# Linear attention block and gated MLP on one core: statistics, loads and issue orders rearranged at the start, in the middle and at the end

## The chip, the cores and the metric

The kernel runs on one core of a Trainium2 chip. A core has TensorE (PE in the profile; PEld are its weight loads), VectorE (DVE), ScalarE (ACT), GpSimd (POOL) and SyncE (SP), each with its own instruction stream; they meet at semaphores. SP and ACT issue the DMAs here. The metric is device time in microseconds, lower is better.

## The reference

The sequence has 2048 tokens of width 512. Two residual blocks follow one another:

```
h   = x + A(layernorm(x))           # layernorm without weights, eps 1e-5
A:    q, k, v = split(xn @ wqkv)    # 32 heads of width 16
      phi(t) = where(t > 0, t + 1, exp(t)) + 1e-6
      o = (phi(q) @ (phi(k)^T v)) / (phi(q) . sum_s phi(k) + 1e-6)
      A = o @ wo
out = h + B(layernorm(h))
B:    z = gelu(hn @ w_in)           # 512 -> 1792, tanh form
      z1 = z[:, :896];  z2 = layernorm(z[:, 896:])
      g = w_sp @ z2 + b_sp          # w_sp is 2048 x 2048 over tokens
      B = (z1 * g) @ w_out          # 896 -> 512
```

## The kernel before, in words

Tokens lie in 16 tiles of 128; four tiles make a group (tg). Everything stays in SBUF. The program first records every operation with its engine, reads and writes (class `_Prog`), and then issues them on each engine in an order that is written out by hand: `ORDER` is a packed list of all operation numbers. So the order of the calls in the code says what depends on what, and the list says when each engine does it. An engine takes its operations strictly in that order, and one that waits holds up all behind it. The matmuls, activations and DMAs go through helpers, so many different operations carry the line of one helper (L402 matmuls, L421 activations, L432 loads, L435 DMA transposes, L533 norms); tiles tell them apart.

**Head.** Pool sets constants, among them `warm`, which the warm-up matmuls read. x is loaded in pieces (x0 is tile 0, x4-5 two tiles), wk is the K third of wqkv in two halves, wq the Q third. `k_unit` handles two tiles: mean and variance of each (`stats`, two DVE operations), `rstd` on Pool (add eps, power -0.5, and for tiles from 6 on the negated mean), the norm, and a transpose to xnT: tiles 0 to 5 by PE (`tr`) and an ACT copy (`cp`), the others by a DMA transpose on SP (`xt`). Then the K product (k0, k1, ...), `phi` to pk (exp on ACT, min and a scalar_tensor_tensor, "stt", on DVE), and the accumulation C += xn^T pk in four PSUM banks (C0, C1, ..., one for each tile). This gives the context matrix with v folded in later: ct is the copy of C, kv multiplies it with wv and masks heads, m multiplies that with wo. `q_unit` makes phi(q) of two of four channel blocks of a group, transposed (pqT). `z_unit` sums pk over tokens (zsum, zsel, zc).

**h stage.** For each group, `den` is the denominator; ACT takes its reciprocal as exp(-ln), SP spreads it over partitions in four DMAs (`spread`), and DVE multiplies pqT by it (`pqmul`). For each tile, h = x + pqT^T m: PE product (h0, h1, ...) in one of three banks, DVE add with the row sum (L726), ACT square with its sum (hSq), Pool `moments` (three operations of 128x1) and power, DVE norm (hn), and a DMA transpose to hnT (ht).

**z stage.** z2 products (z2 0 to 15, one for a tile; gelu on ACT, layernorm) and z1 products (transposed, 7 for a group). w_sp is transposed by DMA in row blocks of 128, whole or as two halves of 1024 columns.

**Gating.** One Strassen step over pairs of token groups (`cell`): DVE combines blocks of w_sp into t and of z2 into s, PE multiplies, DVE gates with z1. `mo` is the output product of a tile, a DVE add of h (L797) and the store.

Of the kernel before, what the change touches and what calls it, by code (L numbers as in the profile page):

```python
# [7 lines left out]
BF16 = mybir.dt.bfloat16  # L8
# [5 lines left out]
EARLY = 2  # L14
SEM_NS = 45.0
ORDER = "c-jTQ1war05Cgz%k0L5!pjZfsf`}+8SQvny7zikW0d{wHcXxMpcXxMpcX#)lGhC1k8ITc~;D*e|f;P$yccg?PlEVQhU;qdq6>`7>X^<A_;fk#AL{8*_7jmO0d=Q9Y2tsj`Ks_X(K1!l4N}~!YAsh0*8+nlrzQ_+h1fw8Ip$y8xAC(b>02DwWG(bZ%Mk7>3G(r%H7*t0`v_~g&Kw-op4n@!mVQ7K~R6`BKBLPn6j4tSk?r4st=z;PmhlQwsa16&tj6hA)!YI^6YIH+S^g>HSq6I3V4ieD{^RWPn&>DNN7j3W)`!O10Fb>Hu7K^b2%div&a1e(u5#!MteXtUJ(GUHx9EULogE0g{F$|M10V}WyZP5->Fd4Hk3&$`OM=%EiFc8P_7)S945Ag);)Ikr>TGKEcb1@HVuo`Qz37atkGqDcqu?1VP4Lh(MCvgHhu?xF#3LCHyr*Q@sa2{uI1?O-PS8)lKaSbo<40rGxH*pKsaRX2B7ccP-js#QiHeTT^UgHZs<1U=|4sY-k_i!H{@g8aU13%$FBPo8sC!}L~{(>`8GZj-Z6EiR)U74KUkc{7vi!SuyZ=~TL1hO>!n1w;i&8#fSJoKgy^U|03S%%Rp&zh`2e->kLmS9O1U^bRz3^Q{hBN@Vi3}7e=(T%~Z$S{^;Ef!`2He@*SaT8mz6=T_n+3C(4^k6A=W=?vtH;1qfhcbdiSeu(!jg8oaTiBY7S)G+wnN8S~b=Zt?Y{Nt*u?7$EFo&@(hjRqSavYCvJmWc^fttnz3{n+#Wm|S*J9cLjCvYLRvM!Hu5f}3qSFj$Nb2?YDsEVrx`>{PcuqWFpfmPXp^;t|Mw1oXRfCD**BUw_VR9eBB!I_-MrQF5c3{e@aVp)ai6i+iu;VP#Hl~<%HsG=&ViYlwBq7<#c?8sgm#nBwYNu12p+{QCJ%RSu7Wt_rUoXzdr!8KgVIh@ONT+een&yL!_d0ft^j8UwrDNfZDuNtbU1l3k8C8~~+bcvT)Uv*Vaw|IrO`G}ACghkXt?bTJ?)k~e#MV-`51Jp<T)l+@dPrcPpuh>Yhd52edjZgWE*Lj!sc!T%(fH(PuZ@G{A`J4y%f}i-AU)VrR^^2z8OeF^;Q)>O;JO1TAKIB2Z<X2wcH@@cwCf9N9q@z;kJDv1{7wN1tN~sfc(Me`dGr20GGRaMul|>NMSlN_aUTUJ;`bl?vWDa@AQ)!h>Ih99}xBQe}{_;^?`Ko{lD!sBQpK>Wcg;ZFhHC!##TqCqli!@$KH9@VkOp~-i1GQaaG)Ut#SW~r1Q#4USv_m^JS-Uh=(=<v$wOAuHT`e?Qd$n9MG)F5nOmj6;v$R@kv|IDERvR^6OSDeEwLp7xK>M^_TeL}=wLu4UNQZSqTeVGRwO>bdO2>3sXLL@NbXn(hMaOkPS9M)CbW^u<LML@ccXdzq^-z!WSWom!&-Fqt^;&QARv+|HpOoJI=$~L2jF!>d%q*Gx&{zG`Fa6aw$-XPOxmpTKZBFK3j^=D>EVE^?l$OeJn~P<&Y?jtOE1hMs?3TlFS|0N;cYCK?=4Bq{Y5C00LaeBTS~2rAZ_97~me&ecuobaV7GdSBpaoixmA2wm!NRPJ1z4n&vl3Rw3R|2-TMdi17>l(^R@tgpHH)$Yd#a1Nrm_}p4^+}B+AF=+7ge|0s%kZ@mesa8mS{=#AF{cVy#"
# [236 lines left out]
def bass_sequential_preLN__linear_attn_block__mixer_gmlp__prompt_kernel(  # L253
# [93 lines left out]
    rc = [g.sbuf(f"rc{b}", o_r + GW * 4 + b * GW * 2, [GW], BF16) for b in range(2)]  # L347
    r16 = [g.sbuf(f"r16{b}", o_xn + b * KD * GW * 2, [KD, GW], BF16) for b in range(NG)]
# [79 lines left out]
    def pool(fn, reads, writes, ns, **k):  # L428
        return g.add("POOL", fn, reads, writes, cost=ns, lat=60, **k)
# [13 lines left out]
    pool(lambda p: p.memset(epst[:, 0:1], EPS_DEN), [], [epst], 80, bias=1e6)  # L443
# [17 lines left out]

    wq = A_wqkv.rearrange("(c p) f -> p c f", p=P)
# [91 lines left out]
    def phi(dst, b, w=2):  # L554

        e, t = e_t[ecnt[0] % NE][:, 0:w, :], psum[:, b:b + w, :]
        ecnt[0] += 1
        act_exp(e, t, ACT.Exp, w * GW)
        dve(lambda v: v.tensor_scalar(e, e, 1.0, EPS_PHI, op0=ALU.min, op1=ALU.add), [e], [e], w * GW, acc=4)  # L559
        dve(lambda v: v.scalar_tensor_tensor(dst, t, 1.0 + EPS_PHI, e, op0=ALU.add, op1=ALU.max),  # L560
            [t, e], [dst], w * GW, ps=True)

    def warmup(n):
# [328 lines left out]
```

## Time and profile before

| what | value |
|---|---|
| median of 5 runs | 236.63 us (236.34 to 237.02) |
| profiled execution, its own time | 237.08 us |
| its span, first to last instruction | 235.2 us |
| PE / DVE / ACT / POOL busy | 227.6 / 150.7 / 92.3 / 54.0 us |
| HBM read / written | 7.47 / 2.10 MB |

A line of the timeline or of the groups gives start, duration in us, engine, line of the kernel, operation, output <- inputs, shape and count; in brackets stands the idle time of the engine before it and what ended it. The chain of waits follows the work that ended last back to the start. The profiled execution is one, the median is of others.

### The profile page before, as it was taken

To read this page: it belongs to the slowest core of one execution; us is meant where nothing else is said; L and a number is where in the kernel's file an instruction comes from. 1 tells how busy PE (TensorE), PEld (TensorE's weight loads), DVE (VectorE), ACT (ScalarE), POOL (GpSimd) and SP (SyncE) were. 2 spreads that over 40 slices of the span, in tenths; PEclk is the share of its full clock that TensorE was granted. 3 is DMA by queue.
4 is the path that set the end of the run, shared out by engine and by line. 5 is a ranking of instruction groups with operands and counts; after the bars stand their busy time and mean duration, and the time that the engine had idled before them with its cause. 6 is when DMAs were issued, how large, how long until landed. Compare 5 with 4: busy or idle time off the path is not lost.

```text
span 235.2 us, 3066 instructions
## 1 busy us (share of the span) xinstructions
PE 227.6 (97%) x1140; PEld 104.6 (44%) x1140; DVE 150.7 (64%) x278; ACT 92.3 (39%) x160; POOL 54.0 (23%) x155
## 2 busy tenths in 40 slices
PE   7699999999999999999999999999999999999994
PEld 7344444453344443444544444444444444444441
DVE  3899755668987543024899989786574055672464
ACT  2568654369689786678942010100001000100000
POOL 4454200000488883007881000000000000000000
DMA  6962379927544347599999600000020000000044
GB/s 202 342 128 60 76 215 355 243 63 175 115 112 89 67 82 99 147 191 186 147 221 227 114 3 0 0 0 0 3 67 0 0 0 3 0 0 0 0 150 143
DMA packets 58687, 23.66 MB, mean 101 GB/s; under 512 B 48433, under 2 KB 58545, under 8 KB 58673
## 3 DMA queue, kind: packets, MB, share of 16 engines
q1 hardware_dynamic: 57840, 22.68, 43.3%
q10 hardware_dynamic: 832, 0.79, 1.1%
q8 instruction: 9, 0.15, 0.3%
q14 instruction: 6, 0.04, 0.1%
HBM read 7.47 MB, written 2.10 MB: 41 GB/s over the span
## 4 chain that ended last, share of the span: by engine, by line
PE 83%; DVE 6%; DMA 4%; POOL 2%; ACT 2%; issue 1%; ACTq 0%
PE psum L402 67%; PE psum L745 6%; PE psum L609 5%; PE psum L748 4%; DMA x<-in_A_x_dram 2%; DMA xnT<-xn 2%; DVE st L503 2%; DVE pqT L560 1%; ACT e L421 1%; DVE pqT L714 1%; POOL st L523 1%; POOL rs L528 1%; DVE h L726 1%; DVE e L559 0%; PE psum L674 0%
## 5 line engine op out<-in xcount | busy, mean ns | idle before, releaser
L402 PE MATMUL psum<-wsp,z 128*128 128x512 bf16 x208 | 47.1, 379 | 0.0
L421 ACT ACTIVATE psum<-psum 128x512 f32<-128x512 f32 x12 | 7.0, 582 | 87.6 <-DVE u L806 44.1
L402 PEld LDWEIGHTS psum<-wsp,z 128*128 128x128 bf16 x208 | 20.2, 98 | 24.8 <-DVE z L533 0.4
L402 PE MATMUL psum<-hnT,win 128*128 128x512 bf16 x112 | 25.6, 379 | 0.0
L402 PE MATMUL psum<-wout,z1T 128*128 128x512 bf16 x112 | 25.3, 379 | 0.0
L806 DVE TENSOR_TENSOR u<-psum,bsp 128x512 bf16<-128x512 f32 x16 | 11.0, 690 | 20.7 <-PE psum L402 20.4
L402 PE MATMUL psum<-t,s 128*128 128x512 bf16 x96 | 21.9, 379 | 0.0
L421 ACT ACTIVATE e<-psum 128x1024 bf16<-128x1024 f32 (+1 forms) x18 | 16.7, 926 | 12.7 <-PE psum L402 12.4
L421 ACT ACTIVATE z1T<-psum 128x512 bf16<-128x512 f32 x28 | 16.4, 594 | 5.9 <-PE psum L402 5.7
L522 POOL TENSOR_SCALAR st<-st 128x1 f32<-128x1 f32 x23 | 5.3, 232 | 51.3 <-ACT sh L421 35.9
L402 PEld LDWEIGHTS psum<-wout,z1T 128*128 128x128 bf16 x112 | 10.9, 97 | 13.3 <-DVE z1T L807 0.5
L745 PE MATMUL psum<-win,hnT 128*128 128x512 bf16 x64 | 16.4, 379 | 0.0
L421 ACT ACTIVATE z<-psum 128x896 bf16<-128x896 f32 x16 | 14.6, 912 | 3.7 <-PE psum L748 3.6
L402 PEld LDWEIGHTS psum<-hnT,win 128*128 128x128 bf16 x112 | 9.8, 97 | 13.6 <-ACT z1T L421 4.4
L402 PE MATMUL psum<-wqkv,xnT 128*128 128x512 bf16 x64 | 15.3, 379 | 0.5 <-ACT xnT L421 0.3
L402 PE MATMUL psum<-m,pqT 128*128 128x512 bf16 x64 | 15.2, 380 | 0.5 <-DVE h L726 0.4
L797 DVE TENSOR_TENSOR h<-psum,h 128x512 bf16<-128x512 f32 x16 | 10.6, 687 | 7.7 <-PE psum L402 7.7
L609 PE MATMUL psum<-pk,xn 128*128 128x512 bf16 x64 | 15.5, 379 | 0.0
L761 DVE BATCH_NORM_STATS2 st<-z 128x6 f32<-128x512 bf16 x9 | 6.1, 682 | 14.4 <-ACT z L421 14.4
L402 PE MATMUL psum<-xnT,wqkv 128*128 128x512 bf16 x64 | 15.3, 380 | 0.0
L402 PEld LDWEIGHTS psum<-t,s 128*128 128x128 bf16 x96 | 9.4, 98 | 11.3
L503 DVE BATCH_NORM_STATS2 st<-x 128x6 f32<-128x512 bf16 x16 | 10.6, 681 | 4.5 <-DMA x<-in_A_x_dram 4.5
(87 smaller groups left out, 321.2 us busy)
## 6 DMA issues: line engine op xcount, KB each, us to landing
r<-rc SPq DMA_DIRECT2D x16, 128.0 KB, 2.7
out_dram<-h SPq DMA_DIRECT2D x16, 128.0 KB, 1.8
win<-in_B_w_in_dram SPq DMA_DIRECT2D x2, 896.0 KB, 5.4
x<-in_A_x_dram SPq DMA_DIRECT2D x5, 256.0 KB, 6.6
wqkv<-in_A_wqkv_dram SPq DMA_DIRECT2D x2, 512.0 KB, 6.3
wout<-in_B_w_out_dram SPq DMA_DIRECT2D x1, 896.0 KB, 8.6
wo<-in_A_wo_dram SPq DMA_DIRECT2D x1, 512.0 KB, 6.6
bsp<-in_B_b_sp_dram SPq DMA_DIRECT2D x1, 512.0 KB, 4.3
```

The source lines that it names most:

```text
L402: inst = pe.matmul(out_ap, lhsT=a, rhs=b, start=start and i == 0, stop=stop and i == len(pairs) - 1, **kw)
L421: return g.add("ACT", lambda ac: ac.activation(out_ap, in_ap, func, **kw), [in_ap, *extra], [out_ap] + ([accum] if accum is not None else []),
L503: dve(lambda v: v.bn_stats(s[:, 0:6], src[:, n, :]), [src[:, n, :]], [s[:, 0:6]], D)
L522: pool(lambda p: p.tensor_scalar(mean, s[:, 0:1], 1.0 / n, None, op0=ALU.mult), [s[:, 0:1]], [mean], 190)
L523: pool(lambda p: p.tensor_scalar(s[:, 2:3], mean, mean, EPS_LN, op0=ALU.mult, op1=ALU.subtract), [mean], [s[:, 2:3]], 240)
L528: pool(lambda p: p.tensor_tensor(r, ve, expo[:, 0:1], ALU.pow), [ve, expo], [r], 620)
L609: inst = pe.matmul(bank(CB[c]), lhsT=xn[:, i, c * P:(c + 1) * P], rhs=pk[:, i, :], start=i == 0, stop=i == NT - 1)
L745: pe.matmul(bank(b), lhsT=hnT[:, c, n * P:(n + 1) * P], rhs=win2[:, c, 0:GW], start=c == 0, stop=c == KD - 1)
L748: inst = pe.matmul(bank(b + 1, F2), lhsT=hnT[:, c, n * P:(n + 1) * P], rhs=win2[:, c, GW:FH], start=c == 0, stop=c == KD - 1)
L761: dve(lambda v, n=n, s=s: v.bn_stats(s[:, 0:6], z2[:, n, 0:GW]), [z2[:, n, 0:GW]], [s[:, 0:6]], GW)
L797: dve(lambda v: v.tensor_tensor(o, bank(b), h[:, n, :], ALU.add), [bank(b), h[:, n, :]], [o], D, ps=True)
L806: dve(lambda v: v.tensor_tensor(t, bank(b), add, ALU.add), [bank(b), add], [t], GW, ps=True)
```

## The change

It edits many places at once:

- Pool's memset of `warm` comes first, and 42 warm-up matmuls take the place of 48.
- x2 and x3 are loaded before wk; x4 to x15 all go on SP, behind a wait for x0.
- The rstds of tiles 0, 2 and 3 are made by ACT as exp(-0.5 ln(v + eps)); the sums of tile 1 by two ACT passes, with Pool's `moments` and power.
- `moments` does the mean last. For h tiles from 2 on, Pool does moments and power for two tiles in one operation each (`moments_pair`), and their two norms follow.
- phi of q30 and q32 (the last group's two halves) is split: t + 1 on ACT, the max on DVE. All four copies ct are on ACT.
- One block of w_sp instead of two is loaded early, before the first DMA transpose of xn (tile 0's block instead of tile 1's). All later ones come in a fixed order.
- The reciprocal buffers are merged in pairs; `MERGE` is empty, so the DMAs stay one for each group and block.
- The last tile's output is made in two halves of 256 columns; the second half is the last work of PE, and its store is issued by ACT.
- The order of all operations is written anew. The scheduling costs in the code (`cost`, `issue`, `lat`) only went into making such lists.

The parts of the two lists that the prediction speaks of, expanded (`bnst` is a stat, `bnag` its aggregate, `min1`, `stt`, `max` the steps of phi):

```
PE  before  warmup, tr x0 x1, k0 k1, tr x2 x3, k2 k3, C0, tr x4 x5, C1, k4 k5 k7, C2, k6, C3 C4 C5, k8 k9
PE  after   warmup, tr x0 x2 x3 x1, k0 k1 k2 k3, C0, tr x4 x5, C1, k4 k5, C2 C3, k6 k7, C4 C5, k9 k8
DVE before  bnst/bnag x0, x1, norm 0, bnst x3, norm 1, bnst x2, bnag x3 x2, bnst x7 x6, bnag x7, norm 2,
            bnag x6, norm 3, bnst x5 x4, min1 k0, bnag x4 x5, min1 k1, stt k0 k1, norm 4 5
DVE after   bnst/bnag x0, bnst x3 x2, bnag x3 x2, norm 0 2 3 1, bnst x6 x7, bnag x6 x7, bnst x4 x5, bnag x4,
            min1 k0, bnag x5, min1 k1, stt k0 k1, norm 4 5
ACT after   ld x1 x3 wk, table, two passes of x1, Ln Exp x0, Ln Exp x2-3, cp 0 2 1 3, exp k0 k1, norm 6
SP  before  x0 wk x2 x4-5 x8.. x14-15 wq, w_sp 1, xt 7 6 8 9 11 10 12 13 15, win1, xt 14, win2, wo, wout,
            w_sp 2b 3b, wv, w_sp 0, spreads
SP  after   x0 x2 wk x4-5 x6-7 .. x14-15 wq, w_sp 0, xt 6 7 9 8 11 10 12 13 14 15, win1, wout, wv,
            w_sp 1a 1b, win2, w_sp 2a, wo, spreads
PE  before  C14, zsum, C15, zsel, q22, den0, kv, den1, q22, m m, q30 q30, m m, den2, q32 q32, h0 h2 h3 h1, den3,
            h5 h4 h6 h7, z2 0, h8 h9 h10 h11, z2 2
PE  after   zsum, C14 C15, zsel, q22, den0, q22, kv, den1, q30 q30, m m, den2, m m, q32 q32, h0 .. h6, den3,
            h7, z2 0, h8 h10 h9 h11, z2 1
DVE after   h0, pqmul, h1 h2 h3, hn0, min1 q32, max q30, max q32, h4, hn1, h5, pqmul x2, hn2, h7 h6, hn3, h8
```

```diff
-EARLY = 2
+EARLY = 1
 SEM_NS = 45.0
-ORDER = "c-jTQ1war05Cgz%k0L5!pjZfsf`}+8SQvny7zikW..."
+ORDER = "c-jTQ13(x66a>(_`&;u?tD)6uwc1+qs)en!Ev*`B..."
...
-    rc = [g.sbuf(f"rc{b}", o_r + GW * 4 + b * GW * 2, [GW], BF16) for b in range(2)]
-    r16 = [g.sbuf(f"r16{b}", o_xn + b * KD * GW * 2, [KD, GW], BF16) for b in range(NG)]
+    rcp = g.sbuf("rcp", o_r + GW * 4, [2, GW], BF16)
+    r16 = [g.sbuf(f"r16{b}", o_xn + b * KD * 2 * GW * 2, [KD, 2, GW], BF16) for b in range(NG // 2)]
...
+    head = len(g.ops)
+    pool(lambda p: p.memset(epst[:, 0:1], EPS_DEN), [], [epst[:, 0:1]], 80, bias=1e6)
+    pool(lambda p: p.memset(epst[:, 1:2], EPS_LN), [], [epst[:, 1:2]], 80, bias=1e6)
+    pool(lambda p: p.memset(epst[:, 2:3], 1.0 + EPS_PHI), [], [epst[:, 2:3]], 80, bias=1e6)
...
+    g.ops[1].soft.add(0)
+    for op in g.ops[head:]:
+        op.soft.add(1)
...
+        if behind is not None:
+            op.deps.add(behind.i)
...
-    load_x("SP", 0, 1, 2650)
-    load_x("ACT", 1, 1, 2850)
+        return op
+
+    def load_x(eng, n, w, lat, behind=None):
+        return first_load(eng, x[:, n:n + w, :], x_d[n * P:(n + w) * P, :], f"x{n}", lat, behind)
+
+    x0 = load_x("SP", 0, 1, 2150)
+    load_x("ACT", 1, 1, 2250)
+    load_x("SP", 2, 1, 2500)
+    load_x("ACT", 3, 1, 2500)
     for eng, c in (("SP", 0), ("ACT", 2)):
-        first_load(eng, wqkv[:, c:c + 2, D:2 * D], A_wqkv[c * P:(c + 2) * P, D:2 * D], f"wk{c}", 4800)
-    load_x("SP", 2, 1, 5300)
-    load_x("ACT", 3, 1, 5300)
-    load_x("SP", 4, 2, 6800)
-    load_x("ACT", 6, 2, 6800)
-    for n, t in ((8, 7600), (10, 8300), (12, 9100), (14, 9900)):
-        load_x("SP", n, 2, t)
-    first_load("SP", wqkv[:, :, 0:D], A_wqkv[:, 0:D], "wq", 11400)
+        first_load(eng, wqkv[:, c:c + 2, D:2 * D], A_wqkv[c * P:(c + 2) * P, D:2 * D], f"wk{c}", 3600)
+    for n, lat in ((4, 2400), (6, 2600), (8, 2800), (10, 3000), (12, 3200), (14, 3400)):
+        load_x("SP", n, 2, lat, x0)
+    first_load("SP", wqkv[:, :, 0:D], A_wqkv[:, 0:D], "wq", 4600)
...
+    def rstd_act(s, r, n, w, col):
+        rr, ve = r[:, n:n + w, :], s[:, n:n + w, col + 1:col + 2]
+        act_exp(rr[:, :, 1:2], ve, ACT.Ln, 80, bias=epst[:, 1:2], extra=[epst[:, 1:2]])
+        act_exp(rr[:, :, 0:1], rr[:, :, 1:2], ACT.Exp, 80, scale=-0.5)
+
     def moments(s, col, n):
 
         mean, ve = s[:, col:col + 1], s[:, col + 1:col + 2]
+        pool(lambda p: p.tensor_scalar(s[:, 2:3], s[:, 0:1], s[:, 0:1], -1.0 / (n * n), op0=ALU.mult, op1=ALU.mult), [s[:, 0:1]],
+             [s[:, 2:3]], 240)
+        pool(lambda p: p.tensor_scalar(ve, s[:, 2:3], s[:, 1:2], EPS_LN, op0=ALU.add, op1=ALU.add), [s[:, 1:3]], [ve], 240)
         pool(lambda p: p.tensor_scalar(mean, s[:, 0:1], 1.0 / n, None, op0=ALU.mult), [s[:, 0:1]], [mean], 190)
-        pool(lambda p: p.tensor_scalar(s[:, 2:3], mean, mean, EPS_LN, op0=ALU.mult, op1=ALU.subtract), [mean], [s[:, 2:3]],
-             240)
-        pool(lambda p: p.tensor_scalar(ve, s[:, 1:2], s[:, 2:3], None, op0=ALU.subtract), [s[:, 1:3]], [ve], 230)
+
+    def moments_pair(i, n):
+        s, r = st[1][:, i:i + 2, :], rs[1][:, i:i + 2, 0:1]
+        mean, m2, ve = s[:, :, 6:7], s[:, :, 2:3], s[:, :, 7:8]
+        pool(lambda p: p.tensor_scalar(mean, s[:, :, 0:1], 1.0 / n, None, op0=ALU.mult), [s[:, :, 0:1]], [mean], 230)
+        pool(lambda p: p.tensor_tensor(m2, mean, mean, ALU.mult), [mean], [m2], 280)
+        pool(lambda p: p.tensor_tensor(ve, s[:, :, 1:2], m2, ALU.subtract), [m2, s[:, :, 1:2]], [ve], 280)
+        pool(lambda p: p.tensor_scalar(ve, ve, EPS_LN, None, op0=ALU.add), [ve], [ve], 230)
+        pool(lambda p: p.tensor_tensor(r, ve, expo[:, 0:2].rearrange("p (a b) -> p a b", b=1), ALU.pow), [ve, expo], [r],
+             740)
 
...
+        if split:
+            act(dst, t, ACT.Identity, w * GW, bias=epst[:, 2:3], extra=[epst[:, 2:3]])
+            dve(lambda v: v.tensor_tensor(dst, dst, e, ALU.max), [dst, e], [dst], w * GW, acc=2)
+        else:
+            dve(lambda v: v.scalar_tensor_tensor(dst, t, 1.0 + EPS_PHI, e, op0=ALU.add, op1=ALU.max),
+                [t, e], [dst], w * GW, ps=True)
...
-    warmup(48)
+        PE(fn, [warm], [bank(7, P)], n * 103, bias=1e6)
+
+    warmup(42)
...
+    ACTS = (1,)
+    QSPLIT, KSPLIT, CACT = (6, 7), (), 2
...
+            if i in ACTS:
+                s = st[0][:, i, :]
+                act(sh_t[0], x[:, i, :], ACT.Identity, D, accum=s[:, 0:1])
+                act(sh_t[1], x[:, i, :], ACT.Square, D, scale=D ** -0.5, accum=s[:, 1:2])
+                moments(s, 6, D)
+                rpow(s[:, 7:8], rs[0][:, i, 0:1])
+            else:
+                stats(x, 0, i)
+                if n == 0:
+                    rstd_act(st[0], rs[0], i, 1, 6)
+        if n == 2:
+            rstd_act(st[0], rs[0], n, 2, 6)
+        elif n:
             rstd(st[0], rs[0], n, 2, 6, n >= HEAD)
...
+                if i == HEAD:
+                    first_xt = g.last
...
-        phi(pqT[:, c:c + 2, tg * GW:(tg + 1) * GW], b)
+        phi(pqT[:, c:c + 2, tg * GW:(tg + 1) * GW], b, 2, 2 * tg + c // 2 in QSPLIT)
...
-        if c % 2:
+        if c % 2 < CACT:
             act(ct[:, c, :], bank(CB[c]), ACT.Copy, GW)
...
+    def spread(tg, c, w):
+        i = tg % 2
+        src, dst = rcp[32 * c:32 * (c + 1), i:i + w, :], r16[tg // 2][:, c, i:i + w, :]
+        src_ap = bass.AP(src.tensor, src.offset, [list(src.ap[0]), [0, 4], [1, w * GW]])
+        g.add("SP", lambda q: q.dma_start(dst, src_ap), [rcp[:, i:i + w, :]], [dst], cost=700, lat=2200, dma=f"r{tg}{c // 2}")
...
+        if n < HPAIR:
+            moments(s, 6, D)
+            rpow(s[:, 7:8], rs[1][:, n, 0:1])
+            done = [n]
+        else:
+            done = [n - 1, n] if n % 2 else []
+            if done:
+                moments_pair(n - 1, D)
+        for i in done:
+            hn = hn_t[i % NH]
+            norm(HN(i), hn, h[:, i, :], st[1], rs[1], i, 6, D)
+            g.last = dma_t(hnT[:, :, i * P:(i + 1) * P], hn, f"ht{i}")
...
+    prev = late
     for i, t in enumerate(order):
         w = NT // 2 if EARLY <= i < NT // 2 else NT
         for j in range(0, NT, w):
-            dma_t(wsp[:, j:j + w, t * P:(t + 1) * P], B_w_sp[t * P:(t + 1) * P, j * P:(j + w) * P], f"wsp{t // TPG}",
-                  issue=520 + 4 * w * 53.5).soft.add(queue["SP"][-1].i if i < EARLY else late.i)
+            op = dma_t(wsp[:, j:j + w, t * P:(t + 1) * P], B_w_sp[t * P:(t + 1) * P, j * P:(j + w) * P], f"wsp{t // TPG}",
+                       issue=5000 if i < EARLY else 1350 if w < NT else 2650)
+            op.soft.add(queue["SP"][-1].i if i < EARLY else prev.i)
+            prev = op if i >= EARLY else prev
+            if i < EARLY:
+                first_xt.soft.add(op.i)
...
+        w = D // 2 if n == NT - 1 else D
+        for j in range(0, D, w):
+            b, cs = MB[n % nb] if j == 0 else 0, slice(j, j + w)
+            o = h[:, n, cs]
+            parts = ((0, 3, 6, 1, 4), (2,), (5,))
+            for i, fcs in enumerate(parts):
+                matmuls(bank(b, w), [(z1T[:, fc, n * P:(n + 1) * P], wout[:, fc, cs]) for fc in fcs],
+                        start=i == 0, stop=i == len(parts) - 1)
+            dve(lambda v, o=o, b=b: v.tensor_tensor(o, bank(b, w), o, ALU.add), [bank(b, w), o], [o], w, ps=True)
+            dma("SP" if j == 0 else "ACT", out_d[n * P:(n + 1) * P, cs], o, f"o{n}{j}", issue=600, lat=2000)
+            g.final.append(f"o{n}{j}")
```

## The prediction

> **What bounds the kernel now.** I read part 1 of the page first, then the busy times by stage, then the chain, then the timeline of the stages where TensorE is not full.
>
> ```profile
> span 235.2 us, 3066 instructions
> PE 227.6 (97%) x1140; PEld 104.6 (44%) x1140; DVE 150.7 (64%) x278; ACT 92.3 (39%) x160; POOL 54.0 (23%) x155
> ```
>
> PE is the bound, but a mean over stages says nothing on where time is to be had. The columns of the next view are PE, PEld, DVE, ACT, POOL busy in each stretch.
>
> ```profile
> 8.50:13.10 4.60, 4.05 (x25) 1.67 (x23) 4.60 (x16) 3.67 (x7) 3.23 (x8) 1.00 1.16 275
> 57.50:71.10 13.60, 12.96 (x61) 5.06 (x60) 12.47 (x32) 10.36 (x25) 7.75 (x22) 1.00 0.51 113
> 71.10:119.90 48.80, 48.80 (x242) 22.40 (x241) 23.25 (x58) 39.11 (x76) 29.25 (x81) 1.00 0.73 130
> 119.90:232.30 112.40, 112.36 (x521) 50.45 (x518) 73.38 (x109) 8.91 (x15) 3.98 (x9) 1.00 0.17 41
> 232.30:235.20 2.90, 0.00 (x0) 0.00 (x0) 0.69 (x1) 0.00 (x0) 0.00 (x0) 1.00 0.40 136
> ```
>
> From 71.1 to 232.3 PE never stops: no edit there can gain, one can only lose. Time is to be had in the head, in the h stage and in the last 2.9 us. From 8.5 to 13.1 DVE is full (4.60 of 4.60). The timeline of the head shows what it does:
>
> ```profile
> 6.31 6.63 SPq L435 DMA_TRANSPOSE wsp<-in_B_w_sp_dram  x1
> 8.57 1.25 DVE L503 BATCH_NORM_STATS2 st<-x 128x6 f32<-128x512 bf16 x2
> 9.82 0.38 DVE L533 TENSOR_SCALAR xn<-x,st,rs 128x512 bf16<-128x512 bf16 x1
> 10.21 0.38 DVE L533 TENSOR_SCALAR xn<-x,st,rs 128x512 bf16<-128x512 bf16 x1
> 12.23 1.28 DVE L560 SCALAR_TENSOR_TENSOR pk<-psum,e 128x512 bf16<-128x512 f32 x2
> 13.09 1.03 PE L609 MATMUL psum<-pk,xn 128*128 128x512 bf16 x4
> 17.38 1.02 PE L402 MATMUL psum<-wqkv,xnT 128*128 128x512 bf16 x4 [0.18 <-DMA xnT<-xn]
> ```
>
> The first product with pk (call it C0, 13.09) waits for pk of tile 0 (12.23 plus 0.68), and that sits behind four stats of x and the norms of tiles 2 and 3 (9.82, 10.21). At 17.38 PE waits for the transpose of a later tile. In the h stage PE waits for DVE:
>
> ```profile
> 61.49 0.40 PE L704 MATMUL psum<-pqT,zc 128*32 128x512 bf16 x4 [0.17 <-DVE pqT L560]
> 62.09 3.80 PE L402 MATMUL psum<-m,pqT 128*128 128x512 bf16 x16 [0.21 <-DVE h L726]
> 70.27 1.04 PE L402 MATMUL psum<-m,pqT 128*128 128x512 bf16 x4 [0.21 <-DVE h L726]
> 34.44 7.75 SPq L435 DMA_TRANSPOSE wsp<-in_B_w_sp_dram  x2
> ```
>
> The last line is for the rival below: two half blocks of w_sp, issued behind loads of win and wo that have not landed, hold SP for 7.75 us; with nothing before them such an issue takes 1.31 (at 72.17).
>
> **What the Trainium skill says.** "TensorE: Matmul & The Clock Gate", Part 1, states that full clock comes after some 3.4 us of activity, whatever the number of matmuls. The trace agrees: warm-up matmuls start 107 ns apart from 1.76 and 54 ns apart from about 5.4. "DMA: Bandwidth & Descriptors", Issuing engines are not separate DMA queues, states that loads from SP and ACT run on the same 16 DMA engines; here they share 342 GB/s in the page's second slice (5.9 to 11.8 us), so a reordered load swaps places with another. "GPSIMD Engine Reference", Specifications, states that GpSimd's SBUF interface is shared with VectorE; a 128x1 op at 65.56 took 1.14 instead of 0.29 beside DVE's two 0.65 us multiplies.
>
> **Part by part.** Issue orders are those of the two packed order strings, expanded.
>
> *Warm-up.* The memset of warm moves from 1.50 to about 0.8; PE starts at 1.05. At 107 ns, 3.6 us to full clock as now, the rest at 54, 42 matmuls end at 5.1. Gain nothing: x0 bounds. The gap to the first transpose (6.4) is 1.3 us; a gap of 1.3 before 7.89 leaves the clock at full now.
>
> *Loads.* x0 and x1 come at 3.6 and 3.4 as now. x2 and x3 land now 5.3 and 5.1 after issue, at 7.0 and 6.8, behind wk. Before wk, half the bytes lie ahead of them: about 4.4. wk lands at 6.2 to 6.8 instead of 5.2, still before its use at 7.9. SP then waits for x0 (3.6) to issue x4-5 and the rest: seven DMAs, 0.5 each and 1.07 for wq, so the first w_sp block is issued at 7.9 and not 6.3. The rings hold 1 MB until past 6, so the DMA engines do not run dry, and x6-7 lands at 8.3 to 8.5 as now (issue 2.21 plus 6.1). The block's issue ends now when wq lands (12.95), and should again, at the worst 1.5 later.
>
> *First rstds.* Tiles 0, 2, 3 leave POOL (about 1.1 a pair) for ACT: Ln and Exp of 128x1 or 128x2. No such row exists; bounds are 0.19 (the accumulator read, 128x1) and 0.3, the price of "ScalarE: Activation LUTs", Rules for kernel authors. I take 0.25. Table load 2.1 to 3.4, two passes over x1 (0.61 each, as sh) to 4.8, Ln and Exp to 5.4, norm x0 at 5.9 behind the stats of x3 and x2; second Ln and Exp to 6.5; norms of tiles 2, 3, 1 to 7.5. Tile 1 goes through POOL's four ops, done by 7.0. First k product about 7.9 instead of 8.1. That alone gains nothing; but norms 2 and 3 are now done before x6-7 lands. DVE starts its full stretch at 8.45, not 8.57, without two norms (0.30 apart each): 0.12 + 0.60 = **0.7 us earlier** at pk 0, thus at C0.
>
> *Does it last?* Everything after it on DVE up to stt k4-5 is the same work, so C4 comes at 20.15, not 20.83. PE now runs C2, C3 ahead of k6; k6 is wanted at 18.1, k7 at 19.0, their transposes land 17.3 to 18.8. Gain kept: **-0.65**.
>
> *ct, z.* All four ct copies on ACT: 4 x 0.54 = 2.2 us, two of them 0.69 each off DVE. PE meanwhile has zsel, q22 and den0, 2.9 us, so kv no longer waits (0.5 now). But h0 needs m, whose copies end an ACT chain (ct, two Ln/Exp, exp q22, exp q30, m): worked out in row durations 9.65 us after C15, now 57.48 - 47.80 = 9.68. Net nothing. ACT's load there becomes 8.06 + 1.1 of 9.7.
>
> *Split phi of q30, q32.* DVE loses two 1.22 us ops for two bf16 max of 0.68 (row of the pq multiply); ACT gains 2 x 1.0. den3 then waits for max q32, about 6.4 after h0; PE reaches it at 6.05, a stall of 0.45, and h7 of 0.3 more. z2 of tile 0 starts 8.25 after h0, exactly as now.
>
> *Pairs.* Two tiles now take 8 POOL ops, 3.3 us; a pair takes 5, about 2.3 (0.23 + 2 x 0.28 + 0.23 + 0.74, 0.1 between). hn3 gains, hn2 waits for its partner. By DVE's order h7 add is 10.2 after h0, h11 ends at 13.2 instead of 13.65: **-0.45**.
>
> *Later orders, rcp, wsp.* The merged reciprocal buffers send the same 16 DMAs. z1 of group 1 wants its four transposes at 27.5 after h0, they land near 25; group 3's last, behind two w_sp halves on SP, at 103 for 105; the last w_sp half lands at 117 to 119 for a combine at about 124. Covered by 2 to 5 us each: nothing. If the cover goes, PE stops for the excess.
>
> *Tail.*
>
> ```profile
> 232.30 0.69 DVE L797 TENSOR_TENSOR h<-psum,h 128x512 bf16<-128x512 f32 x1 [0.22 <-PE psum L402]
> ```
>
> With half a tile last, this add is 0.69 - 256/0.96 ns = 0.42. Seven products become fourteen of half the width, 14 x 109 ns against 7 x 216. The 64 KB go out on idle ACT (issue 0.39 against 0.33). **-0.25**, between -0.1 and -0.5.
>
> **Sum.** -0.65 - 0.45 - 0.25 = -1.35. Of the profiled execution's 237.08 (span 235.2) this leaves 235.7. That execution lies 0.45 above the median 236.63, so I forecast 235.3.
>
> **Rivals.** *wo comes late (slower).* SP's order after the last x transpose becomes win1, wout, wv, two halves of w_sp, win2, one half, wo. That transpose is later too: the stats of x14 now stand behind stt q00, its norm is ready at 32, so win1 is issued near 35.3 (now 30.09). 2.3 MB at 342 GB/s, begun 1.5 to 2.5 us after the issue, land by 43.6 to 44.6, and the w_sp halves hold SP until then. win2 follows, another half holds SP until 46 to 49.5, wo lands between 51 and 54. The first m product wants it at 53.2. Nearly no slack. From 53.2 on each us late is a us of PE; at 54.7 all gain is gone, at 56.5 the kernel takes about 238.6. For it: the 7.75 us row. Against: the third half has only one load before it. *The head doesn't move (about 236.0).* x6-7 lands 0.7 later as its issue is now 4.2 and not 2.2, or ACT's small ops take 0.3 or more with waits, and norm 2 and 3 end in DVE's full stretch again; the other terms stay. *The head gains more (about 234.4).* If x4 to x7 land near 7.6, DVE starts its full stretch when norm 1 ends: up to 0.9 more; for it, DMA moves only 202 GB/s in the page's first slice, 342 in the second. *ACT as bound of the h stage (236.5 to 237).* With 2.0 added ACT is busy 12.4 of 13.6; if its waits push max q32 by 1 us, den3, h7 and h8 follow.
>
> **Chances.** Forecast as worked out 0.40; more in the head 0.16; head still 0.14; ACT as bound 0.12; wo late 0.18 (half of it slower than now, half only less gain). Faster by over 0.2% are the first two, 0.11 of the head that stays still and a little of wo late: 0.69. Within 0.2% lie half of ACT as bound, the rest of the still head and some of wo late: 0.15. Slower is the remainder, 0.16; 0.2% (0.47 us) is about what a measurement of this kernel tells from no change. Range 233.9 to 237.1: the best head with the best tail below; wo or ACT giving the gain back above.
>
> **What would show it.** Right: C0 near 12.4, DVE's stats of x6 starting at about 8.4 with both norms before it; z2 of tile 0 about 8.2 after h0; kv without a wait; last DVE add 0.42; PE full from h11 to the end. Wrong: a wait of the m products (L402, psum<-wo,kvm) on a DMA, C0 at 13 or later, den3 over 1 us late, or any PE gap after 71.

## The result, and the profile after

| | median | executions | range |
|---|---|---|---|
| changed | 236.63 us | 44 | 235.64 to 239.62 |
| before, same chip | 236.75 us | 79 | 236.26 to 238.96 |

The ratio is 0.9997, 95% interval 0.9986 to 1.0009: no difference, where 235.3 was forecast. (Ratios leave out disturbed executions; medians and ranges are over all.) The middle 90% of the changed kernel's executions lie between 235.84 and 239.0, those of before between 236.38 and 237.76: the good ones are better than before's, the bad ones worse. In 14 of the changed kernel's 44 the mean granted clock is 0.992 or 0.993; their median is 237.66, that of the other 30 is 236.33.

The profiled execution shows nearly the whole promised gain. Its page:

```profile
span 234.1 us, 3061 instructions
...
PE 227.4 (97%) x1141; PEld 105.9 (45%) x1141; DVE 147.3 (63%) x275; ACT 97.1 (41%) x172; POOL 45.6 (19%) x134
```

Its own time is 235.81, that of before's profile 237.08: 1.27 less, and the sum had said 1.35. But 235.81 lies 0.8 below its kernel's median, and 237.08 lies 0.3 above before's. Two single executions, a lucky one and an unlucky one, bear out a forecast that the medians refute. The busy times by stage (PE, PEld, DVE, ACT, POOL, then clock, DMA share, GB/s):

```profile
8.50:13.10 4.60, 3.55 (x18) 1.40 (x16) 4.55 (x13) 2.88 (x7) 2.60 (x6) 1.00 1.05 311
47.20:57.20 10.00, 9.21 (x65) 4.39 (x63) 4.92 (x12) 8.37 (x15) 0.00 (x0) 1.00 0.99 271
57.20:70.60 13.40, 12.98 (x63) 5.49 (x62) 11.75 (x32) 12.80 (x28) 5.98 (x14) 1.00 0.49 95
70.60:119.00 48.40, 48.40 (x241) 22.48 (x239) 23.28 (x58) 38.51 (x77) 23.50 (x68) 1.00 0.59 111
119.00:231.50 112.50, 112.48 (x529) 51.42 (x527) 73.11 (x110) 9.14 (x16) 3.64 (x8) 1.00 0.24 55
231.50:234.10 2.60, 0.00 (x0) 0.00 (x0) 0.42 (x1) 0.00 (x0) 0.00 (x0) 1.00 0.26 80
```

From 70.6 to 231.5 PE is full, as before. In the h stage ACT is now busier (12.80) than DVE (11.75). The second row is the one to look at: PE works 9.21 of 10 us while the DMA engines are full (0.99). In the kernel before they were half empty in that stage:

```profile
47.80:57.50 9.70, 9.46 (x66) 4.61 (x66) 6.56 (x14) 8.06 (x13) 0.00 (x0) 1.00 0.46 108
```

First the head, from the timeline of all engines:

```profile
5.71 0.38 DVE L555 TENSOR_SCALAR xn<-x,st,rs 128x512 bf16<-128x512 bf16 x1
...
6.40 1.06 DVE L555 TENSOR_SCALAR xn<-x,st,rs 128x512 bf16<-128x512 bf16 x3 [0.31 <-ACT rs L421]
...
6.92 5.81 SPq L435 DMA_TRANSPOSE wsp<-in_B_w_sp_dram  x1
...
8.55 1.29 DVE L510 BATCH_NORM_STATS2 st<-x 128x6 f32<-128x512 bf16 x2 [1.09 <-DMA x<-in_A_x_dram]
...
11.67 1.28 DVE L586 SCALAR_TENSOR_TENSOR pk<-psum,e 128x512 bf16<-128x512 f32 x2
```

All four first norms are done by 7.5, DVE then waits 1.09 us for x6-7, and its full stretch starts at 8.55 without a norm in it: pk of tile 0 at 11.67, C0 at 12.41 (forecast 12.4), C4 at 20.18 (forecast 20.15). Then SyncE's queue and TensorE in the stage of the second row:

```profile
37.48 8.35 SPq L435 DMA_TRANSPOSE wsp<-in_B_w_sp_dram  x2
45.88 0.58 SPq L432 DMA_DIRECT2D win<-in_B_w_in_dram  x1
46.50 1.24 SPq L435 DMA_TRANSPOSE wsp<-in_B_w_sp_dram  x1
47.78 0.57 SPq L432 DMA_DIRECT2D wo<-in_A_wo_dram  x1
```

```profile
53.91 0.59 PE L402 MATMUL psum<-wo,kvm 128*128 128x512 bf16 x2 [0.55 <-DMA wo<-in_A_wo_dram]
...
57.41 0.81 PE L402 MATMUL psum<-m,pqT 128*128 128x512 bf16 x3
```

The same two steps in the kernel before:

```profile
33.27 0.56 SPq L432 DMA_DIRECT2D wo<-in_A_wo_dram  x1
...
52.32 0.60 PE L402 MATMUL psum<-wo,kvm 128*128 128x512 bf16 x2
```

Two half blocks of w_sp hold SyncE for 8.35 us, so wo is issued at 47.78 (33.27 before) and lands at 53.77. PE could have started the products that make m (psum<-wo,kvm) at about 53.2, and waits. (Such a time counts the last product before it with its 216 ns to the next start; the idle time in brackets counts from an end that the profile models, and is 0.17 shorter.) That is why h0 starts at 57.41: only 0.07 before the 57.48 of before, although C4 is 0.65 earlier. The h stage and the tail then give what they should. The end of the chain of work:

```profile
231.50 0.02 issue
231.52 0.42 DVE h L855
```

### The profile page after: what moved, and what is told of

Same layout as the page of the kernel before. It is cut to its first block, busy times and chain, and to the rows that moved or that the text cites. A ratio compares the mean times of both kernels' runs of the same rounds, so it can differ in the third digit from the quotient of the medians.

```text
span 234.1 us, 3061 instructions
## 1 busy us (share of the span) xinstructions
PE 227.4 (97%) x1141; PEld 105.9 (45%) x1141; DVE 147.3 (63%) x275; ACT 97.1 (41%) x172; POOL 45.6 (19%) x134
## 4 chain that ended last, share of the span: by engine, by line
PE 81%; DMA 6%; SPq 5%; ACT 3%; DVE 3%; issue 1%; POOL 1%
PE psum L402 66%; PE psum L796 6%; PE psum L799 4%; SPq L435 4%; PE psum L649 4%; DMA x<-in_A_x_dram 3%; DMA wo<-in_A_wo_dram 3%; SPq L432 1%; ACT e L421 1%; DVE st L510 1%; ACT m L421 1%; DVE h L770 0%; DVE e L581 0%; PE psum L569 0%; ACT rcp L421 0%
## 5 line engine op out<-in xcount | busy, mean ns | idle before, releaser
L402 PE MATMUL psum<-wout,z1T 128*128 128x512 bf16 (+1 forms) x119 | 25.2, 366 | 0.0
L402 PEld LDWEIGHTS psum<-wout,z1T 128*128 128x128 bf16 x119 | 11.7, 98 | 12.8 <-DVE z1T L865 0.5
L855 DVE TENSOR_TENSOR h<-psum,h 128x512 bf16<-128x512 f32 (+1 forms) x17 | 10.8, 657 | 6.9 <-PE psum L402 6.9
L799 PE MATMUL psum<-win,hnT 128*128 128x384 bf16 x64 | 13.0, 326 | 0.0
L770 DVE SCALAR_TENSOR_TENSOR h<-psum,x 128x512 bf16<-128x512 f32 x16 | 10.8, 687 | 3.2 <-PE psum L402 3.2
```

Source lines behind the costliest of these rows:

```text
L402: inst = pe.matmul(out_ap, lhsT=a, rhs=b, start=start and i == 0, stop=stop and i == len(pairs) - 1, **kw)
L770: dve(lambda v, n=n, b=b, s=s: v.scalar_tensor_tensor(h[:, n, :], bank(b), 1.0, x[:, n, :], op0=ALU.mult, op1=ALU.add, accum_out=s[:, 0:1] ...
L799: inst = pe.matmul(bank(b + 1, F2), lhsT=hnT[:, c, n * P:(n + 1) * P], rhs=win2[:, c, GW:FH], start=c == 0, stop=c == KD - 1)
L855: dve(lambda v, o=o, b=b: v.tensor_tensor(o, bank(b, w), o, ALU.add), [bank(b, w), o], [o], w, ps=True)
```

## The experiments

**Theory.** The edits gain at least what the sum said; two of their side effects take it back: wo lands late, as in the profile, in the other executions too, and 42 warm-up matmuls leave TensorE's clock in the head to chance. **Rivals.** The gains are smaller than the two traces say, since one execution was compared with one; or the time goes elsewhere, as in the transposes of h.

Each ratio is to the kernel before on the same chip. Medians of the kernel before differ by up to 0.5 us from chip to chip, so runs on one chip are the ones to compare. "wo first" is one move in SyncE's order:

```diff
 SP: ld win1; ld wout; ld wv;
+    ld wo;
     dmaT wsp1[0:8]; dmaT wsp1[8:16]; ld win2; dmaT wsp2[0:8];
-    ld wo;
```

### Each repair alone, and both

```diff
-    warmup(42)
+    warmup(56)        # e1, e3, k3, all g, l2
+    warmup(24)        # e4, l1
     SP order          # wo first in e2, e3, k2, all c (but c5), all g, l1, l2
```

First chip.

e1_warm56: 

> The changed kernel with 56 warm-up matmuls instead of 42, nothing else. In the changed kernel's profile all 42 start 107 ns apart and end at 5.5 us without reaching the full clock, and 14 of its 44 runs show a granted clock of 0.993 with a median of 237.7 us, against 236.3 for the 30 others. Theory W (warm-up too short): with 14 more, activity lasts to 6.3 to 7.0 us, the share of runs at 0.993 falls from a third to under a tenth, and the median falls by 0.3 to 0.6 us, to 236.0 to 236.3 against 236.7 before. Theory R (the clock falls later, in the gaps of the head, whatever the warm-up): share and median stay. Theory N (the spread is wo landing at different times): the share stays a third or does not matter, median within 0.1 of the changed kernel.

e2_wo_first: 

> The changed kernel with one DMA moved: wo is issued right after wv, ahead of the two w_sp halves and of win2. In the profile PE waits 0.7 us for wo at 53.0 to 53.9. If wo is on the path: the m products start at about 53.2, the end comes 0.6 to 0.7 us earlier, median about 236.0, and the spread of the runs at full clock shrinks. If wo's wait is absorbed later (h0 waits for the m copies on ACT anyway): 0 to 0.2 us. The share of runs at clock 0.993 should stay about a third under theory W.

e3_warm56_wo: 

> Both edits, 56 warm-up matmuls and wo right after wv. If the two causes are separate, the gains add: median about 235.4 to 235.7, which is the time that was forecast (235.3), at a clock of 1.000 in nearly all runs. If only one of them is real, the median equals that one's run.

e4_warm24: 

> The changed kernel with 24 warm-up matmuls instead of 42; PE is busy from 1.0 to 3.6 us and then idle to 6.1. Theory W: nearly all runs show 0.993 or less, the k products of the first tiles start 427 ns apart instead of 216 in the profile, and the median is 237.3 or more. Theory R or N: no change beyond 0.2 us, and the share of runs at low clock stays a third.

| first chip | median | ratio, 95% |
|---|---|---|
| e1: 56 warm-ups | 236.04 | 0.9963, 0.9945 to 0.9980 |
| e2: wo first | 235.26 | 0.9924, 0.9898 to 0.9950 |
| e3: both | 235.38 | 0.9921, 0.9893 to 0.9950 |
| e4: 24 warm-ups | 236.61 | 0.9995, 0.9975 to 1.0016 |

Second chip, the changed kernel beside its two repairs, and the short warm-up put into the kernel before:

k1_after: 

> The changed kernel itself, as the measure for the two beside it. Level with the kernel before, as in the first comparison: a ratio of 0.997 to 1.001. In the profile, the products with m wait for wo by 0.7 us or more.

k2_wo: 

> The changed kernel with wo loaded right after wv. Theory: wo lands before 53 and its wait goes; 0.7 to 1.7 us less than the changed kernel beside it, so a ratio of about 0.992. If the wait was of the two profiled executions only and not of the others, less than 0.3 us.

k3_warm56: 

> The changed kernel with 56 warm-up matmuls in the place of 42, nothing else. Theory: the clock is full when the first transposes start and stays so; 0.3 to 0.5 us less than the changed kernel beside it, and fewer runs above 237.3. If VectorE alone sets C0, so that the products before it may run at any clock: no difference.

k4_before34: 

> The kernel before with 34 warm-up matmuls instead of 48, so that TensorE's warm-up ends at about 5.4 us, a gap of 1 us ahead of the first transpose as in the changed kernel. Theory: its clock then is not safe either, and it gets 0.3 to 1.0 us slower, with runs spread further above the median. If the warm-up has no part in the result: within 0.2 us of the kernel before.

| second chip | median | ratio, 95% |
|---|---|---|
| k1: changed kernel | 236.81 | 0.9980, 0.9959 to 1.0002 |
| k2: wo first | 235.86 | 0.9931, 0.9905 to 0.9957 |
| k3: 56 warm-ups | 236.06 | 0.9960, 0.9935 to 0.9985 |
| k4: before with 34 warm-ups (of 48) | 237.53 | 1.0013, 0.9986 to 1.0040 |

wo first is worth 0.95 us here (k1 to k2, intervals apart) and 0.66 with 56 warm-ups on the other chip (e1 to e3, intervals just meeting). With this one load moved and nothing else, the ratio is 0.9924 and 0.9931 on two chips; the forecast, 235.3 of 236.63, is 0.9944. So undoing one step brings the gain that was forecast.

The longer warm-up alone gives 0.75 (k1 to k3), but the intervals overlap, and with wo first it gave nothing (e2 to e3, 0.12 the other way). e4 missed what was expected of it: its median is 236.61 and not 237.3 or more, and 2 of its 22 executions show a clock of 0.993, not nearly all. k4 decides nothing: 0.4 above in medians, its interval holds 1.

Executions with a mean granted clock of 0.993 or less are 18 of 88 of the changed kernel (14 of 44, 1 of 22, 3 of 22), 5 of 40 with 56 warm-ups, 2 of 16 with wo first, and none of 18 with both (e3, g1, l2). That goes with two causes, but most of the 18 belong to one measurement, so it does not settle what part the warm-up has.

In k1 TensorE waits 1.8 us for wo in all, where the first profile had 0.55; the landing of wo varies between executions:

```profile
PE psum L402 <- DMA wo<-in_A_wo_dram: 1.8, 1, 1.8
```

| execution | wo lands | first product that makes m | end of C15 to h0 |
|---|---|---|---|
| before | 39.83 | 52.32 | 9.66 |
| changed | 53.77 | 53.91 | 10.23 |
| c5, k1 (the same kernel) | 54.70, 55.26 | 54.84, 55.39 | 11.28, 11.46 |
| k3 (56 warm-ups) | 54.96 | 55.10 | 12.82 |
| k2, g1 (wo first) | 47.98, 47.84 | 53.66, 53.31 | 9.56, 9.58 |

In the twelve profiled executions with wo first the last column lies between 9.54 and 10.00, around the 9.65 of the prediction; in the six with wo late it lies between 10.23 and 12.82. The execution of k3 shows the worst case, in its busy times by stage:

```profile
53.00:56.00 3.00, 1.31 (x8) 0.23 (x6) 0.56 (x1) 0.49 (x1) 0.00 (x0) 1.00 1.07 336
56.00:60.00 4.00, 3.85 (x14) 1.34 (x11) 2.23 (x4) 3.69 (x7) 0.00 (x0) 0.57 0.42 111
60.00:64.00 4.00, 4.00 (x20) 1.84 (x19) 2.83 (x8) 3.19 (x6) 1.08 (x4) 1.00 0.57 128
```

PE does 1.31 of 3 us while it waits for wo, and then the granted clock is 0.57 in the mean of 4 us: products start up to 427 ns apart instead of 216. From the first product that makes m to h0 it takes 4.94 us, where the first profile has 3.50, so this costs another 1.4 us. The wait is paid nearly twice; that execution took 238.29 where its kernel's median is 236.06.

### The changed kernel again, and parts of it undone

c5_after: 

> The changed kernel, unedited, on the chip that the other three of this set use, as their base. If its low clock (14 of 44 runs at 0.993) belongs to the kernel, about a third of the runs here show it too and the median is about 236.6. If it belongs to the chips or the hour, nearly no run shows it and the median is 235.9 to 236.1, near the one with 56 warm-up matmuls (236.04).

c6_wo_nohalf and c7_wo_nosplit have wo first, and the tail or the split of phi undone; c8_wo_xlate has wo first and wk loaded ahead of x2 and x3:

```diff
-            w = D // 2 if n == NT - 1 else D                # c6
+            w = D
-    QSPLIT, KSPLIT, CACT = (6, 7), (), 2                    # c7
+    QSPLIT, KSPLIT, CACT = (), (), 2
+    wk loads                                                # c8
     load_x("SP", 2, 1, 2500); load_x("ACT", 3, 1, 2500)
-    wk loads
```

c6_wo_nohalf: 

> wo right after wv, and the last tile's output in one piece of 512 columns again (its place in the order stays, tile 14 is last). Against the run with wo right after wv alone (235.26): the prediction's tail term says 0.25 slower (0.1 to 0.5), as the last add grows from 0.42 to 0.69 us and the store goes through SP. If the second queue (ACT) costs as much as the half saves, no difference.

c7_wo_nosplit: 

> wo right after wv, and phi of q30 and q32 in the old form: one scalar_tensor_tensor on DVE behind each min, no ACT pass. Against wo right after wv alone (235.26): the prediction called the split neutral. If ACT is the bound of the h stage (12.80 of 13.4 us busy in the changed kernel), taking 2.0 us off ACT gains 0.3 to 0.8. If DVE is, putting 1.1 us back on it loses 0.3 to 0.8. Within 0.2 if both hide.

c8_wo_xlate: 

> wo right after wv, and the wk halves loaded ahead of x2 and x3 again; the rest of the head as changed. Against wo right after wv alone (235.26): x2 and x3 land at 6.8 to 7.0 instead of 4.0 to 4.3, DVE's stats of them and norms 2 and 3 fall into its full stretch again, so pk of tile 0 and C0 come at 13.1 or later instead of 12.4 to 12.9 and the time grows by 0.6 to 0.9. If the head's gain came from the ACT rstds and not from the loads: no change.

Measured, all on one chip: c5 236.38, ratio 0.9981 (0.9964 to 0.9997); c6 235.86, 0.9956 (0.9943 to 0.9970); c7 236.24, 0.9965 (0.9951 to 0.9979); c8 237.78, 1.0036 (1.0022 to 1.0050). c6, c7 and c8 lie above the 0.992 to 0.993 that wo first gave elsewhere, so each part that was undone seems to gain; but no run with wo first alone stands beside them, and the intervals of c6 and c7 overlap with those on other chips. c8 is clear of them, yet it measures more than the order of loads. The changed order of DVE has the norm of tile 0 behind the stats of tiles 2 and 3, which land at 6.19 and 6.39 in c8's profile (4.04 and 4.27 in the first one). So DVE waits, the first transpose starts at 8.28, 2.6 us after the warm-up, the first k products run at half speed and C0 starts at 15.33. What the loads are worth without that order was not measured. In c7's busy times by stage DVE is the fuller engine again and the stage is a microsecond longer than the 13.13 that g1 below takes:

```profile
56.77:70.90 14.13, 12.94 (x61) 5.26 (x62) 12.96 (x33) 10.22 (x23) 4.88 (x14) 1.00 0.49 102
```

c5's execution shows another loss. Timeline of PE:

```profile
75.17 1.04 PE L402 MATMUL psum<-m,pqT 128*128 128x512 bf16 x4 [0.59 <-DVE pqT L758]
```

h14 waits for pqT of group 3, whose reciprocals are spread late: SyncE's transpose of tile 1 of h took 2.43 us to issue and not 1.19, and the copies stand behind it. PE starts h14 0.76 us late. The profiles of c6, c8, e4 and l1 (below) show the same, with this issue at 1.94 to 2.36 us and h14 0.3 to 0.8 us late: five of the ten profiled executions with the new orders and 42 or 24 warm-ups. None of the eight with 56 warm-ups shows it; there tile 1's transpose is issued in 1.19 us, and a later one, the tenth or eleventh, takes 1.78 to 2.47. Why the long issue moves is open.

### On top of both repairs

g1_base is e3 again; beside it one part is moved or undone each time, all on a third chip.

```diff
 SP: dmaT ht1; spread31; spread30;                           # g2
-    dmaT ht2;
     spread32; spread33;
+    dmaT ht2;
-            w = D // 2 if n == NT - 1 else D                # g3
+            w = D
-    AB, HPAIR = [4, 5, 7], 2                                # g4
+    AB, HPAIR = [4, 5, 7], 16
```

g1_base: 

> The changed kernel with 56 warm-up matmuls and wo loaded right after wv, as in the run that had both: the measure for the three runs beside it. If the two repairs account for what was lost, it takes 235.2 to 235.7 us, 0.991 to 0.995 of the kernel before. If that earlier run was luck of one chip, it lies near 236.2 and above 0.996. At 0.991 to 0.995 the profile shows no wait of the products with m on wo; a stall of h14 on the reciprocals of group 3 may or may not be in it.

g2_ht2late: 

> As the run before it in this list, but SyncE issues the transpose of tile 2 of h after the four copies of group 3's reciprocal and not between them. Theory A (a transpose's issue takes 2.4 us instead of 1.2 in part of the executions, and the copies behind it come too late for h14): the reciprocals land 1.2 us earlier, h14 never waits, and the median drops by up to 0.4 us, the share of executions times the 0.76 us seen; the transposes of tiles 2 and 3 land up to 1.4 us later, before z1 of group 0 wants them. Theory B (the long issue comes late in few executions, or the later transposes delay z1 of group 0): no difference within 0.2, or slower by up to 0.7 with a wait of z1 on hnT in the profile.

g3_nohalf56: 

> As the first of this list, but the last tile is done whole, as in the kernel before. The term of the prediction for the tail: 0.25 us slower, between 0.1 and 0.5; the last add takes 0.69 instead of 0.42 in the profile. If the halves cost as much in TensorE's fourteen short products as they save at the end: no difference.

g4_nopairs56: 

> As the first of this list, but each tile of h has its own four moment operations on GpSimd (eight for two tiles instead of five). The prediction's term for the pairs: h11 ends about 0.45 us later after the start of h0, so 0.45 us slower. Rival: GpSimd waits for the squares anyway, h8 and later h products wait for VectorE's adds and products with the reciprocal, and the time stays within 0.2 us.

| third chip | median | ratio, 95% |
|---|---|---|
| g1: both repairs | 234.91 | 0.9892, 0.9865 to 0.9918 |
| g2: tile 2's transpose later | 234.96 | 0.9899, 0.9877 to 0.9922 |
| g3: last tile whole | 235.79 | 0.9939, 0.9915 to 0.9963 |
| g4: no pairs | 235.63 | 0.9931, 0.9907 to 0.9955 |

With both repairs the kernel takes 2.3 us less than before on that chip. g2 equals g1. But g1's profile shows no stall of h14, as none with 56 warm-ups does, so this says nothing of the kernel with 42: there the stall stays a possible part of the loss. The tail is worth 0.9 by medians (0.45 by the traces: from PE's last start to the end 2.84 us in g1, 3.40 in g3, less the 0.11 by which the last product is shorter), the pairs 0.7; the intervals of g1 to g3 and of g1 to g4 overlap a little, so the sizes are rough, but every execution of g3 and g4 is slower than every one of g1. The place of the second is seen in the timeline of PE in g4:

```profile
67.55 2.76 PE L402 MATMUL psum<-m,pqT 128*128 128x512 bf16 x12 [0.81 <-DVE h L770]
```

Without pairs an h product waits 0.81 us for an add. On DVE that add stands behind the norm of tile 2 of h (66.47), which itself waits 0.83 us for the reciprocal root of its moments from POOL; in g1 the same norm waits for nothing. The same stage in g1 and g4, by stage:

```profile
56.87:70.00 13.13, 12.69 (x61) 5.43 (x62) 12.15 (x33) 12.54 (x27) 5.98 (x14) 1.00 0.49 106
```

```profile
56.25:70.30 14.05, 12.72 (x61) 5.44 (x62) 12.24 (x33) 13.45 (x28) 8.54 (x21) 1.00 0.49 107
```

### The price of a cold head

l1_wo24: 

> wo right after wv and only 24 warm-up matmuls, so that the clock of the head is cold in every execution. Theory: the products of the first k tiles run at 427 ns for some 3 us, C0 starts at 12.9 instead of 12.4, and the median lies 0.4 to 0.6 us above the run beside it; then 42 warm-ups, cold in about three executions of seven, cost some 0.2 us. Rival: a cold head leads on to a clock that stays low longer and costs 1 us or more. If VectorE hides it: less than 0.2 us.

l2_wo56: 

> wo right after wv and 56 warm-up matmuls: the head is never cold. The measure for the run beside it; 0.989 to 0.993 of the kernel before, as in its two earlier runs.

l1 took 236.41, ratio 0.9998 (0.9970 to 1.0026); l2 234.84, 0.9917 (0.9887 to 0.9947), on one chip: 1.6 us, the rival's side. In the timeline of PE of l1 the transposes (16 in 2.18 us) and the first k products run cold, in l2 they do not:

```profile
6.26 2.18 PE L569 MATMUL psum<-ident,xn 128*128 128x128 bf16 x16 [2.48 <-DVE xn L555]
8.24 4.43 PE L402 MATMUL psum<-wqkv,xnT 128*128 128x512 bf16 x16
12.56 0.60 PE L649 MATMUL psum<-pk,xn 128*128 128x512 bf16 x2
```

```profile
6.94 1.04 PE L569 MATMUL psum<-ident,xn 128*128 128x128 bf16 x12 [0.27 <-DVE xn L555]
7.82 3.62 PE L402 MATMUL psum<-wqkv,xnT 128*128 128x512 bf16 x16
11.65 0.60 PE L649 MATMUL psum<-pk,xn 128*128 128x512 bf16 x2 [0.21 <-DVE pk L586]
```

C0 is 0.91 later in l1, and 0.41 of that is x6-7, which landed at 8.19 there and at 7.78 in l2. So the cold clock makes C0 0.5 later in this pair. The pair differs by 0.93 in the end, but 0.42 of that is the stall of h14, which l2 does not have; h0 itself is only 0.41 later. So of the 1.6 the cold products explain about 0.5 at most, as far as this pair shows; six of l1's fourteen executions took 237.4 or more, and the profiled one is not among them. The rest stays open.

A cold head does not cost the same each time. In all twelve profiled executions that have the changed order of loads and a warm head, C0 follows the landing of x6-7 by 3.87 or 3.88 us. Of seven with 42 warm-ups and that order of loads three were cold in the head; of eight with 56 none. In e2 and k2 the distance is 4.73 and 4.17; in c6 it is 3.88, as in e4: DVE hid the cold products, and c6's late C0 (12.91) is that of a late landing (9.03). Three sevenths of 1.6 is 0.7, an upper estimate of what 42 warm-ups cost.

e4, cold in the head but with wo late, is no slower than the changed kernel. Where C0 is late, the wait for wo can cover it, as wo lands no later for it; that is argued and not shown. The gains of the two repairs at any rate do not add up (e1, e2, e3).

## Why the prediction was wrong, by its own steps

One step decided: the landing of wo. The prediction put it between 51 and 54 us, left the wait out of its forecast, and gave it 18% as a rival. It came at 53.8 to 55.3 with a warm head, always after the need, and moving that load back brings the forecast gain.

- **Loads, First rstds, Does it last?** Held in the profiled pair. Ln and Exp took 0.28 and 0.20 for one tile, 0.30 and 0.21 for two (0.25 was taken); C0 and C4 came within 0.03. One step was off without effect: the first block of w_sp was issued at 6.92, not 7.9. But the head hangs on landings that the sum took as fixed. In the changed kernel C0 follows the landing of x6-7 by 3.88 us (8.53 and 12.41; 8.80 and 12.68 in k1). In the kernel before it follows that of x3, from which on DVE has no gap, by 6.29 (6.80 and 13.09; 6.04 and 12.32 in k4). x6-7 landed between 7.78 and 9.03 with the changed order of loads, x3 differs by 0.76 between those two executions: each moves more than the 0.7 that was to be gained. On the second chip the changed kernel's C0 (k1) is even later than that of k4.
- **Warm-up, "Gain nothing".** The step "3.6 us to full clock as now" failed. All 42 matmuls of the profiled execution started 107 ns apart, the last at 5.39, where the end had been put at 5.1 with the last ones at 54. With the same start full speed came after 2.7 us in k2 and after 5.6 in g3. In k2 the warm-up ended at 4.8, and a gap of 1.5 us lost the full clock again. The prediction took the 3.6 us of one trace, and its gap of 1.34 which the clock survived, for constants. What this costs in the median is not resolved: between nothing (e2 to e3) and 0.75 (k1 to k3).
- **ct, z, "Net nothing".** Held: 9.54 to 10.00 from C15 to h0 where wo is early.
- **wo comes late.** The rival that decided, given 18%. Its mechanism, its place and its price were right (in k1 wo lands 1.80 us after PE could use it, and h0 comes 1.81 later than the 9.65); the step that failed is the landing: "land by 43.6 to 44.6 ... wo lands between 51 and 54". win1, wout and wv had landed only by 45.99. The DMA engines were full (share 1.07 from 37.2 to 46.0) but moved 286 GB/s, not the 342 of the head: 366 from 40 to 43, then 190 from 43 to 46, where 714 of 1097 packets were under 512 bytes. Nearly all are so while a transpose of xn runs (586 of 609 from 35 to 37.2), so these are taken for the packets of the w_sp transposes. win2 was issued at 45.88 and wo at 47.78. It landed at 53.8 to 55.3 in all five profiled executions with wo late and the head warm, where PE could have used it at 53.1 to 53.5. A landing whose middle lay 0.7 ahead of the need was no 18% case; put off by the 2 us that the loads ahead of it were late, it was the likeliest. That a wait of this size can also cost the clock, and with it another 1.4 us, was not foreseen.
- **Split phi, Pairs (-0.45).** Right in sign and, together, nearly in size: h11 ends 13.06 after h0 (13.2 forecast, 13.66 before). Singly each was under-sized: without the split the stage is 14.12 long, without the pairs 14.05, in an order that was made for both. In the first DVE is the fuller engine, in the second DVE waits for POOL: two bounds side by side, of which taking one away alone gains nothing here. z2 of tile 0 came 7.9 after h0, not 8.25.
- **Later orders, "Covered by 2 to 5 us each".** No wait was seen on what it names. It left out the spread of group 3's reciprocals, which had no cover in c5, c6, c8, e4 and l1 (0.3 to 0.8 us). Whether that moves the median with 42 warm-ups is open.
- **Tail (-0.25).** Right in sign, under-sized: -0.4 by the traces of before and after, -0.45 by those of g3 and g1, at the upper end of the -0.1 to -0.5 that were allowed. The last add took 0.42, as worked out. The medians of g1 and g3 are 0.9 apart, and the other half of that stays open.
- **Sum.** "That execution lies 0.45 above the median" was carried over as a constant. It is one draw from a spread of a microsecond, and the changed kernel's spread is wider than before's. That the profiled pair came near the sum is luck in part: C0 is 0.68 earlier, the h stage 0.60 and the tail 0.50 shorter, and 0.57 of that went to the wait for wo.

So with both repairs the edits gain 1.5 to 2.3 us (0.989 to 0.992 in g1, e3 and l2), more than the sum of 1.35. The late wo takes back 0.66 and 0.95 by the medians on two chips. The rest lies with the head's clock, up to 0.7, with the stall of h14 and with the landings; how it divides can't be told. The split, the pairs, the tail and the loads were undone one at a time; the rstds on ACT, the copies ct and the earlier memset were not.

## What to carry to other kernels

When an edit moves a load behind others in a queue, work out its landing with the rate of the traffic that will really be beside it, and if the landing's range reaches the need, take the wait as the forecast and not as a rival. A head that is tuned to one trace is tuned to one draw of landings and of the clock: keep the warm-up running until the first real product can start (with 56 matmuls none of eight heads was cold), rather than as short as the trace allows. When one part of an order made by hand is undone, as in c8, the rest of that order no longer fits, and the loss is not that part's worth alone. And compare a forecast with medians; a second trace that agrees with it is one execution.

## What the runs showed of the hardware that was not expected

- With warm-up matmuls from 1.04 us on, the first ones 56 ns apart came after 2.7 us (k2) to 5.6 us (g3). With 42 of them full speed was not reached before they ended in six of eight profiled executions.
- A DMA transpose of a 128x512 tile was issued by SyncE in 1.19 to 1.31 us in most cases, but one of the sixteen of h took 1.78 to 2.47 in most executions (that of tile 1 in c5, c6, c8, e4 and l1, that of tile 0 in e2, c7 and k2, a later one in the eight with 56 warm-ups), which delays all that stands behind it.
- An idle time of TensorE of 1.69 us in mid-kernel was followed by products up to 427 ns apart instead of 216 for over 3 us (k3); one of 1.76 at the same place in k1 and one of 1.58 in c5 were not. In the head, 1.15 us after full speed left the clock (c5), 1.51 lost it (k2).
- A head whose warm-up never reached full speed, and whose first products ran cold, shows a mean granted clock of 1.000 in the records all the same (e2, l1): it is seen in the distances of the matmuls, not in that mean. A stretch at half clock that follows after full speed is seen: k3's, of over 3 us, makes the mean 0.993.
- The two last stores landed 1.6 and 1.7 us after their issue in the changed kernel's profile, but 3.4 and 3.7 in e4's, where the stretch after the start of TensorE's last product was 4.6 us long, and 2.8 there. This was seen in one of the twenty profiled executions.
